# Attention times V in two groups of three head pairs per tile instead of three groups of two, with one eviction for each group

## The chip, the cores and the metric

The kernel runs on one core of a Trainium2 chip. The core has five engines that run at the same time, each through its own queue of instructions in order: TensorE (PE, matrix products; its weight loads are shown as PEld), VectorE (DVE), ScalarE (ACT), GpSimd (POOL) and SyncE (SP, which here only issues DMA transfers). Products land in PSUM, which has eight banks of 128 partitions by 512 fp32 columns; another engine has to copy ("evict") them to SBUF before the bank can be used again. The metric is the device time of one execution in microseconds (us); lower is better.

## What is computed

The reference is a chain of three stages over 4 batches, 12 heads, 448 positions and 64 elements per head:

```python
scores = scale * np.matmul(q, k.transpose(0, 1, 3, 2))
scores = np.einsum('bhij,hg->bgij', scores, w_pre)      # heads mixed
attn = softmax(scores)                                   # over j
attn = np.einsum('bhij,hg->bgij', attn, w_post)          # heads mixed again
x = np.matmul(attn, v)                                   # to 1792 tokens x 768
...                                                      # top-1 mixture of 8 experts, 768 -> 1024 -> 768
...                                                      # h = x @ w_in; (h - tanh(h)) @ w_out
```

The change lies in the last product of the attention, `attn @ v`.

## The kernel before

**Tiles and blocks.** Each batch is cut into four tiles of 120, 120, 120 and 88 query rows, so there are 16 tiles T = 0 to 15, all 12 heads together. A tile is cut into blocks of ten query rows times twelve heads, which fill 120 partitions: 12 blocks in a wide tile, 9 in a narrow one (T = 3, 7, 11, 15), 180 in all. Block s belongs to one step s of the loop over blocks.

**One step.** At step s the program issues, in this order: evictions that were left over from the last step (`flush`); P(s), the mixing of heads before the softmax, on TensorE; the maximum over each row on VectorE (L371); the scaled post-mixing matrix w of block s-1 (`emit_W`, L381 to L384, VectorE); at most one "fill" on TensorE (below); the exponential of block s on ScalarE (L374); on some steps a piece of the conversion of the last stage's weights (L115 to L117 on VectorE, L118 to L120 on POOL); T(s-2), the mixing after the softmax together with a transposition, on TensorE (L406), and its eviction on ScalarE (L411); then the other fills of the step. A step with no fill is called bare below.

**Fills.** The rest of the attention's TensorE work is put on given steps by hand: `emit_S2` (scores of two head pairs, for the tile after next), `tr_q` and `tr_k` (transpositions of q and k, split into two fp32r halves by ScalarE and VectorE), `emit_AV2` (attention times V) and `emit_X` (a product that lays a tile's result out as tokens and gives the router's logits). `at(pos, ...)` sets a fill on step int(pos); `at_e` takes the next step that no other fill of bank "e" has. P has two banks ("b"), T two ("c", which the router's small products also use), `emit_S2` takes four banks ("a" as two, "d", "e"), AV has the one bank "d", and tr_q, tr_k and X share the one bank "e". `run_fill` leaves the evictions of AV, tr_q, tr_k and X for later: those of "d" go to ScalarE just before T's eviction of the same step, or at the start of the next step if the fill stood behind T; those of "e" at the start of the next step.

**Attention times V.** For tile T and one pair of heads, eight fp32 products (four chunks of 112 positions, two heads, one in each half of the array's columns) write 128 partitions by 120 (88) columns of bank "d". A profile shows each fp32 product as two records. Two pairs make a group of 32 records with one eviction of 128x240 (128x176). With f the first block of tile T+1, the groups for pairs 0, 2 and 4 stand on steps f+3, f+7 and f+11 if tile T+1 has twelve blocks, on f+3, f+6 and f+9 if it has nine (`posAV`, LAG is 2). The last tile's AV comes after the loop, pair by pair, and is not touched by the change.

**What hangs on those places.** X of tile T goes on the first free steps from one and two steps behind the last group. For each batch (and for the last batch in two parts) the router's work `emit_R` follows X(T, 1) at fixed distances: part 0 (VectorE), then parts 1 and 2 (small products; positions in their queue on VectorE, up to L525), then parts 3 and 4 (small products; sums on VectorE). The store of a tile's tokens is issued on SP's queue behind X's eviction, among the relays L354 that bring scores from one layout to the other eight steps ahead.

**The last steps.** From step 173 on the first expert's weights are loaded, and on steps 175 to 178 they are split (`do1`): a cast on VectorE (L637) and a subtraction on POOL (L639). After the loop come the last X and AV products, the last router group, the experts and the two dense layers.

Of the kernel before, what the change touches and what calls it, by code (L numbers as in the profile page):

```python
# [30 lines left out]
def body(ctx: ExitStack, tc, q, k, v, w_pre, w_post, emb, tau, w1, w2, win, wout, out):  # L31
    nc = tc.nc
    pe, act, dve, pool, sp = nc.tensor, nc.scalar, nc.vector, nc.gpsimd, nc.sync
# [6 lines left out]
    NP = H // 2  # L40
# [13 lines left out]
    def ps(tag, nm):  # L54
        if len(PB) > 1:
            tag = {"a": "h", "b": "h"}.get(tag, "o")
        return psum[-1].tile([128, 512], F32, tag=tag, name=nm, bufs=PB[-1][tag])
# [67 lines left out]
    if True:  # L125
# [165 lines left out]
        def tr_q(T, hf, tag="e"):  # L291
            n = IT[T % 4][1]
            src = nat["q", T]
            pt = ps(tag, f"ptq{T}_{hf}")
            for p in range(3):
                pp = 3 * hf + p
                pe.transpose(pt[:, p * 120:p * 120 + n], src[:n, 2 * pp:2 * pp + 2, :].rearrange("p h d -> p (h d)"), ident[:n, :n])
            pv = pt[:, :360].rearrange("p (c i) -> p c i", c=3)[:, :, :n]
            hi = ap.tile([128, 3, 120], F32R, tag=f"qh{hf}", name=f"qh{T}_{hf}", bufs=1)
            lo = ap.tile([128, 3, 120], F32R, tag=f"ql{hf}", name=f"ql{T}_{hf}", bufs=1)  # L300
            qT[T, hf] = (hi, lo)

            def evac():
                act.copy(hi[:, :, :n], pv)
                return lambda: dve.tensor_sub(lo[:, :, :n], pv, hi[:, :, :n].bitcast(F32))
            return evac
# [56 lines left out]
        def emit_P(i):  # L363
            n = 12 * blocks[i][2]
            t = sr.pop(i)
            pt = ps("b", f"P{i}")
            pe.matmul(pt[:n, :S], wpre[:n, :n], t[:n, :], start=True, stop=True)  # L367

            flush2()
            mx = a2.tile([120, 4], F32, tag="mx", name=f"mx{i}", bufs=5)  # L370
            dve.tensor_reduce(mx[:n, 0:1], pt[:n, :S], op=ALU.max, axis=AX.X, negate=True)  # L371
            p = a2.tile([120, S], F32, tag="p", name=f"p{i}", bufs=LAG + 1)
            pj[i] = (p, mx)
            return lambda: act.activation(p[:n, :], pt[:n, :S], AF.Exp, bias=mx[:n, 0:1], scale=1.0, accum_out=mx[:n, 1:2])  # L374
# [3 lines left out]
        def emit_W(i):  # L378
            n = 12 * blocks[i][2]
            p, mx = pj[i]  # L380
            dve.tensor_scalar_add(mx[:n, 2:3], mx[:n, 1:2], 1e-9)  # L381
            dve.reciprocal(mx[:n, 3:4], mx[:n, 2:3])
            w = a2.tile([120, 120], F32, tag="w", name=f"w{i}", bufs=3)
            dve.tensor_scalar_mul(w[:n, :], wpost[:n, :], mx[:n, 3:4])  # L384
            wj[i] = w
# [4 lines left out]
        def emit_T(i):  # L390
            T, r, m = blocks[i]
            n = 12 * m
            b, it = divmod(T, 4)
            if r == 0:
                A[T] = aA.tile([CP, NJ, H, 120], F32, tag="A", name=f"A{T}", bufs=2)
            p, mx = pj.pop(i)
            w = wj.pop(i)
            wv = w.rearrange("p (g i) -> p g i", i=10)[:n, :, :m]
            pt = ps("c", f"T{i}")
            pv = pt[:CP, :NJ * n].rearrange("p (c g i) -> p c g i", c=NJ, i=m)  # L400
            tev[i] = (pt, pv, p, w, wv, n, m)
# [7 lines left out]
        def emit_TE(i):  # L409
            T, r, m = blocks[i]  # L410
            act.copy(A[T][:, :, :, 10 * r:10 * r + m], tev.pop(i)[1])  # L411
# [3 lines left out]
        def emit_AV(T, p, cpy=act.copy, m=1):  # L415
            b, it = divmod(T, 4)
            n = IT[it][1]
            if p == 0:
                xT[T] = cp.tile([128, KD, 120], F32, tag="xT", name=f"xT{T}", bufs=2)
            pt = ps("d", f"AV{T}_{p}")  # L420
            for x in range(m):
                for c in range(NJ):
                    for hh in range(2):
                        pe.matmul(pt[64 * hh:64 * hh + 64, x * 120:x * 120 + n], vt[b, p + x][:, hh, c, :],  # L424
                                  A[T][:, c, 2 * (p + x) + hh, :n], start=c == 0, stop=c == NJ - 1)
            return lambda: cpy(xT[T][:, p:p + m, :n], pt[:, :m * 120].rearrange("d (x i) -> d x i", x=m)[:, :, :n])
# [8 lines left out]
                e1()  # L435
            return evac

        def emit_AV2(T, p):
            return emit_AV(T, p, act.copy, 2)

        ssk = cp.tile([128, 4 * B], F32, name="ssk")
        lk = cp.tile([128, 4 * B, E], F32, name="lk")
# [171 lines left out]
    with mctx:  # L614
# [240 lines left out]
        def at(pos, fn, *a):  # L855
            side.setdefault(int(pos), []).append((fn, a))
# [3 lines left out]
        def at_e(pos, fn, *a):  # L860
            pos = int(pos)
            while pos in eused:
                pos += 1
            eused.add(pos)
            at(pos, fn, *a)
            return pos
# [5 lines left out]
        def posS2(T, p):  # L872
            return posS(T, p - p % 2 + 0.5)

        def posAV(T, p):
            f, nb = first[T + 1], ntile[T + 1]
            return f + LAG + 1 + p * nb / 6
# [17 lines left out]
        for b in range(1, B):  # L895
            for p in range(NP):
                e = posS2(4 * b - 1, p) + 1
# [3 lines left out]
            for b in range(B):  # L901
                at(posAV(4 * b - 1, p) + 2 if b else 1 + p, load_v, b, p)
        for T in range(4 * B - 1):
            for p in range(0, NP, 2):
                at(posAV(T, p), emit_AV2, T, p)
            e = posAV(T, NP - 2)
            if T == 4 * B - 2:
                continue
            at_e(e + 1, emit_X, T, 0)
            e = at_e(e + 2, emit_X, T, 1) - 2  # L910
            for gi, (_, t1) in enumerate(RG[:-1]):
                if t1 == T + 1:
                    for x, y in enumerate((0, 2, 2, 4, 4)):
                        at(e + 5 + y, emit_R, gi, x)
# [24 lines left out]
        def relay_to(i):  # L939
            while nxt[0] <= min(i, NBK - 1) and blocks[nxt[0]][0] in sdone:  # L940
                emit_relay(nxt[0])
                nxt[0] += 1
# [4 lines left out]
        def flush(tag=None):  # L947
            keep = []
            while late:
                x = late.pop(0)  # L950
                if tag in (None, x[0]):
                    y = x[1]()
                    if x[0] == "e" and callable(y):
                        late2.append((x[0], y))
                else:
                    keep.append(x)
            late.extend(keep)
            if tag:
                flush2(tag)
# [7 lines left out]
                    x[1]()  # L967

        def run_fill(fn, a):
            tag = "d" if fn is emit_AV2 else "e"  # L970
            if fn is emit_S2:
                flush("d")
                flush("e")
            elif fn is not emit_S:
                flush(tag)
            e = fn(*a)
            if fn in (emit_S, emit_S2):
                e()
                if a[1] + (fn is emit_S2) == NP - 1:
                    sdone.add(a[0])  # L980
            else:
                late.append((tag, e))
# [18 lines left out]
        prep_w()  # L1001
        relay_to(NSR - 1)
        at_e(4, tr_en)
        PEF = (tr_q, tr_k, emit_S, emit_S2, emit_AV2, emit_X, tr_en)
        for fn in [f() for f in (tr_q(1, 0, "e"), tr_q(1, 1, "d"))]:
            fn()
        for p in range(3):
# [5 lines left out]
        for s in range(NBK + LAG + 6):  # L1013
            todo = side.get(s, [])
            fill = [x for x in todo if x[0] in PEF]
            for fn, a in todo:
                if fn in (load_q, load_k, load_v, conv_load, zero_fill):
                    fn(*a)
            flush()
            relay_to(s + NSR - 1)  # L1020
            ex = emit_P(s) if s < NBK else lambda: None
            if 0 <= s - 1 < NBK:
                emit_W(s - 1)
            for fn, a in todo:
                if fn is emit_R and a[1] in (0, 1, 3):
                    fn(*a)
            i = s - LAG
            on = 0 <= i < NBK
            fill.sort(key=lambda x: x[0] not in (emit_S, emit_S2, emit_AV2))
            if fill and fill[0][0] in (emit_S, emit_S2, emit_AV2):  # L1030
                run_fill(*fill.pop(0))
            ex()
            for fn, a in todo:
                if fn is conv_do:
                    fn(*a)
            if on:
                emit_T(i)
                T_mm(i, 0, NJ)
                flush("d")
                emit_TE(i)  # L1040
            for x in fill:
                run_fill(*x)
            for fn, a in todo:
                if fn in (to_experts, do1) or fn is emit_R and a[1] in (2, 4):
                    fn(*a)
# [334 lines left out]
```

## Time and profile before

| | |
|---|---|
| median of 3 runs | 1373.29 us (1369.13 to 1375.64) |
| the profiled execution: its own time | 1376.32 us |
| the profiled execution: its span, first to last instruction | 1374.6 us |
| mean granted TensorE clock, as a share of full speed | 0.977 |
| TensorE busy over the span | 96% |
| VectorE, ScalarE, POOL busy | 74%, 54%, 37% |

The steps of the attention run from 24 us to about 518 us of the span. "Busy" of TensorE counts the time from a product's start to its modelled end; products overlap, so lengths of steps are best read from the starts of successive P products, not from busy times.

### The profile page before, as it was taken

Reading aid. Unit: us, or ns where it says so; the run is one execution under the profiler, and the core shown is the slowest. Engines: PE = TensorE matmul, PEld = TensorE weight load, DVE = VectorE, ACT = ScalarE, POOL = GpSimd, SP = SyncE. Lnnn points to the kernel's source line nnn. Section 1 sums busy time; section 2 is a strip of 40 time slices with the busy share of each in tenths; the row PEclk is TensorE's granted clock in tenths of the full one; section 3 lists DMA queues with packets and bytes.
Section 4 is the critical chain, followed back from the end, with each engine's and each line's share of the span. In section 5 each row is a group of like instructions: output and inputs, shape, how many; then the busy total and the mean of one; then the engine's idle time right before and its main releaser. Section 6 shows DMA issues by size and latency. Waiting matters only on the chain. (4 is left out here: it accounts for less than half of the span.)

```text
span 1374.6 us, 24956 instructions
## 1 busy us (share of the span) xinstructions
PE 1312.8 (96%) x9104; PEld 1146.0 (83%) x9104; DVE 1017.7 (74%) x2189; ACT 736.7 (54%) x1518; POOL 502.8 (37%) x495
## 2 busy tenths in 40 slices
PE   7999999999999987999999997899999989999998
PEld 5777776776777766999999996699998889999998
DVE  4776787678677773677776764688888788788886
ACT  5666666675666653545444453554444444544441
POOL 0233333333333323333332422544454334444432
PEclk9999999999999997999999999799999999999999
DMA  6886675667556564778877872421113133121102
GB/s 153 247 253 190 185 209 168 170 201 202 160 173 204 164 205 147 263 253 262 273 233 238 254 220 84 136 69 47 46 48 109 37 96 107 67 61 55 47 24 81
DMA packets 149412, 210.90 MB, mean 153 GB/s; under 512 B 54022, under 2 KB 109494, under 8 KB 149286
## 3 DMA queue, kind: packets, MB, share of 16 engines
q1 hardware_dynamic: 145104, 194.19, 46.4%
q0 software_dynamic: 2640, 12.19, 2.8%
q10 hardware_dynamic: 1542, 2.89, 0.7%
q8 instruction: 73, 1.20, 0.4%
q14 instruction: 53, 0.43, 0.1%
HBM read 135.70 MB, written 35.00 MB: 124 GB/s over the span
## 5 line engine op out<-in xcount | busy, mean ns | idle before, releaser
L406 PEld LDWEIGHTS T<-w,p 120*112 120x112 f32 (+1 forms) x1440 | 166.4, 177 | 66.8 <-issue 44.5
L120 POOL TENSOR_TENSOR cm<-cm,ct 128x256 f32<-128x256 f32 x96 | 70.1, 731 | 404.9 <-DVE ct L117 360.9
L406 PE MATMUL T<-w,p 120*112 120x120 f32 (+1 forms) x1440 | 185.6, 272 | 6.2 <-DVE w L384 3.0
L374 ACT ACTIVATE p<-P,mx 120x448 f32<-120x448 f32 x180 | 114.0, 633 | 119.8 <-DVE mx L381 106.3
L1220 POOL TENSOR_TENSOR gl<-th,gh 128x448 fp32r<-128x448 f32 x64 | 74.8, 1169 | 261.0 <-ACT gh L1219 192.6
L367 PE MATMUL P<-sr,wpre 120*120 120x448 f32 x360 | 166.2, 544 | 1.4 <-ACT p L374 1.4
L1271 PE MATMUL o<-woh,gh 128*128 128x384 f32 x448 | 152.5, 340 | 5.3 <-DVE acc L1277 5.3
L1240 ACT ACTIVATE u<-h 128x448 f32<-128x448 f32 x64 | 34.9, 546 | 222.9 <-PE h L1236 219.2
L1272 PE MATMUL o<-wol,gh 128*128 128x384 f32 x448 | 150.7, 336 | 0.0
L1273 PE MATMUL o<-woh,gl 128*128 128x384 f32 x448 | 150.7, 336 | 0.0
L371 DVE TENSOR_REDUCE mx<-P 120x1 f32<-120x448 f32 x180 | 111.4, 619 | 49.4 <-PE P L367 48.6
L1236 PE MATMUL h<-yh,wil 128*128 128x448 f32 x384 | 143.8, 374 | 3.3 <-POOL wil L1209 3.3
L1234 PE MATMUL h<-yh,wih 128*128 128x448 f32 x384 | 144.0, 375 | 1.1 <-ACT wih L1208 0.6
L1277 DVE TENSOR_TENSOR acc<-acc,o 128x384 f32<-128x384 f32 x196 | 106.9, 548 | 51.4 <-PE o L1273 51.4
L1235 PE MATMUL h<-yl,wih 128*128 128x448 f32 x384 | 143.9, 375 | 0.5 <-DVE yl L1183 0.5
L411 ACT COPY A<-T 112x480 f32<-112x480 f32 x180 | 101.5, 564 | 16.2 <-PE T L406 15.6
L686 PE MATMUL hi<-xhi,w1hi 128*128 128x256 f32 x384 | 108.8, 283 | 0.0
L687 PE MATMUL hi<-xli,w1hi 128*128 128x256 f32 x384 | 108.6, 283 | 0.0
L688 PE MATMUL hi<-xhi,w1li 128*128 128x256 f32 x384 | 108.4, 282 | 0.0
L424 PEld LDWEIGHTS AV<-A,v 112*64 112x64 f32 x1536 | 74.8, 138 | 23.9 <-issue 10.5
L669 PE MATMUL ypi<-w2hi,hhi 128*128 128x384 f32 x272 | 93.2, 343 | 0.1
L670 PE MATMUL ypi<-w2li,hhi 128*128 128x384 f32 x272 | 92.1, 338 | 0.6 <-DVE w2li L639 0.3
(223 smaller groups left out, 3279.9 us busy)
## 6 DMA issues: line engine op xcount, KB each, us to landing
sr<-ssb SPq DMA_DIRECT2D x176, 210.0 KB
r<-in_moe_w SPq DMA_DIRECT2D x72, 384.0 KB
r<-in_moe_w SPq DMA_DIRECT2D x52, 512.0 KB
craw<-in_moe_w_in SPq DMA_DIRECT2D x48, 256.0 KB
craw<-in_moe_w_out SPq DMA_DIRECT2D x48, 256.0 KB
raw<-wi_d SPq DMA_DIRECT2D x15, 768.0 KB
wor<-wo_d SPq DMA_DIRECT2D x15, 768.0 KB
wi_d<-cm SPq DMA_DIRECT2D x48, 128.0 KB
```

The lines of the kernel that those rows point to most:

```text
L367: pe.matmul(pt[:n, :S], wpre[:n, :n], t[:n, :], start=True, stop=True)
L371: dve.tensor_reduce(mx[:n, 0:1], pt[:n, :S], op=ALU.max, axis=AX.X, negate=True)
L374: return lambda: act.activation(p[:n, :], pt[:n, :S], AF.Exp, bias=mx[:n, 0:1], scale=1.0, accum_out=mx[:n, 1:2])
L406: pe.matmul(pt[:CP, c * n:(c + 1) * n] if m == 10 else pv[:, c], p[:n, c * CP:(c + 1) * CP], w[:n, :] if m == 10 else wv, start=True, stop ...
L686: pe.matmul(pt[:, :256], wh[:, sl], xh[:, c, :], start=c == 0, stop=False)
L687: pe.matmul(pt[:, :256], wh[:, sl], xl[:, c, :], start=False, stop=False)
L1234: pe.matmul(pt[:, :S], wi[0][:, c, sl], yh[:, c, :], start=c == 0, stop=False)
L1235: pe.matmul(pt[:, :S], wi[0][:, c, sl], yl[:, c, :], start=False, stop=False)
L1236: pe.matmul(pt[:, :S], wi[1][:, c, sl], yh[:, c, :], start=False, stop=c == KD - 1)
L1271: pe.matmul(pt[:, :384], gh[:, sl], wo[0][:, f, n0:n0 + 384], start=f == 0, stop=False)
L1272: pe.matmul(pt[:, :384], gh[:, sl], wo[1][:, f, n0:n0 + 384], start=False, stop=False)
L1273: pe.matmul(pt[:, :384], gl[:, sl], wo[0][:, f, n0:n0 + 384], start=False, stop=f == GF - 1)
```

## The change

The groups of attention times V take three pairs of heads each: 48 records into 360 of bank "d"'s 512 columns, and one eviction of 128x360 (128x264). A tile has two groups, for pairs 0 and 3, on steps f+3 and f+9 if tile T+1 has twelve blocks, on f+3 and f+7 if it has nine. The same products are issued in the same order. As the last group stands two steps earlier (at f+9 for f+11, or f+7 for f+9), X starts from two steps earlier too, and so does the router's work where X moved. The loads of v keep their steps.

```diff
-        def emit_AV2(T, p):
-            return emit_AV(T, p, act.copy, 2)
+        def emit_AV3(T, p):
+            return emit_AV(T, p, act.copy, 3)
...
         for T in range(4 * B - 1):
-            for p in range(0, NP, 2):
-                at(posAV(T, p), emit_AV2, T, p)
-            e = posAV(T, NP - 2)
+            for p in range(0, NP, 3):
+                at(posAV(T, p), emit_AV3, T, p)
+            e = posAV(T, NP - 3)
             if T == 4 * B - 2:
                 continue
             at_e(e + 1, emit_X, T, 0)
             e = at_e(e + 2, emit_X, T, 1) - 2
```

The other lines of the diff put the new name in the place of the old one where `run_fill` and the loop tell kinds of fills apart.

## Rows read from the trace of the kernel before

**Rows 1.** The page, busy us (share of the span) and instructions by engine

```profile
PE 1312.8 (96%) x9104; PEld 1146.0 (83%) x9104; DVE 1017.7 (74%) x2189; ACT 736.7 (54%) x1518; POOL 502.8 (37%) x495
```

**Rows 2.** Busy time by window: length, PE, PEld, DVE, ACT, POOL, clock, DMA, GB/s

```profile
24.00:480.00 456.00, 449.79 (x3855) 332.16 (x3856) 337.50 (x1049) 306.01 (x728) 155.31 (x216) 1.00 0.67 195
497.60:518.00 20.40, 15.77 (x141) 12.50 (x140) 16.41 (x42) 7.66 (x19) 9.40 (x4) 0.92 0.77 266
```

**Rows 3.** Groups by line and shape: xcount, busy us, mean ns, idle before

```profile
L426 ACT COPY xT<-AV 128x240 f32<-128x240 f32 x36 | 12.7, 353 | 11.2 <-PE AV L424 11.2
L462 ACT COPY raw<-X 120x384 f32<-120x384 f32 x24 | 11.6, 483 | 1.6 <-PE X L458 0.8
```

**Rows 4.** Timeline of PE, steps 174 (with AV) and 175 (bare): start, us

```profile
494.05 0.92 PE L367 MATMUL P<-sr,wpre 120*120 120x448 f32 x2
494.89 1.86 PE L424 MATMUL AV<-A,v 112*64 112x120 f32 x32
496.69 1.07 PE L406 MATMUL T<-w,p 120*112 120x120 f32 x8
497.60 0.92 PE L367 MATMUL P<-sr,wpre 120*120 120x448 f32 x2
...
499.17 0.92 PE L367 MATMUL P<-sr,wpre 120*120 120x448 f32 x2
```

**Rows 5.** Timeline of weight loads: step 53, bare, before T; step 68, before AV

```profile
163.40 0.79 PEld L406 LDWEIGHTS T<-w,p 120*112 120x112 f32 x7 [0.20 <-issue]
...
202.41 1.63 PEld L424 LDWEIGHTS AV<-A,v 112*64 112x64 f32 x32 [0.66 <-issue]
```

**Rows 6.** Timeline of PE, P of steps 54 (with S2) and 55

```profile
164.21 0.92 PE L367 MATMUL P<-sr,wpre 120*120 120x448 f32 x2
...
167.38 0.92 PE L367 MATMUL P<-sr,wpre 120*120 120x448 f32 x2
```

**Rows 7.** Timeline of DVE, steps 33 and 52: maximum, w, conversion, a slow w

```profile
106.55 0.62 DVE L371 TENSOR_REDUCE mx<-P 120x1 f32<-120x448 f32 x1 [0.94 <-PE P L367]
...
107.47 0.28 DVE L384 TENSOR_SCALAR w<-wpost,mx 120x120 f32<-120x120 f32 x1
...
108.44 0.42 DVE L117 SCALAR_TENSOR_TENSOR ct<-craw,ct 128x256 int32<-128x256 int32 x1
...
161.74 0.69 DVE L384 TENSOR_SCALAR w<-wpost,mx 120x120 f32<-120x120 f32 x1
```

**Rows 8.** Timeline of PE around bank "e", steps 24, 34 and 35

```profile
79.15 0.94 PE L367 MATMUL P<-sr,wpre 120*120 120x448 f32 x2
...
80.75 0.55 PE L281 MATMUL ptk<-ident,natk 112*128 112x112 f32 x4
...
107.47 0.92 PE L367 MATMUL P<-sr,wpre 120*120 120x448 f32 x2
...
109.42 0.60 PE L281 MATMUL ptk<-ident,natk 112*128 112x112 f32 x4 [0.21 <-DVE ql L305]
...
112.32 0.46 PE L324 MATMUL S<-kh,qh 64*120 64x448 f32 x1 [0.53 <-DVE kl L288]
```

**Rows 9.** Timeline around the second router group, P of steps 111 and 112

```profile
320.57 0.18 DVE L517 TENSOR_TENSOR pos<-R,carry 128x32 f32<-128x32 f32 x1
...
321.84 1.60 DVE L525 TENSOR_SCALAR p<-iota_s,posk 128x256 f16<-128x256 f32 x4
321.98 0.92 PE L367 MATMUL P<-sr,wpre 120*120 120x448 f32 x2
...
326.55 0.92 PE L367 MATMUL P<-sr,wpre 120*120 120x448 f32 x2
```

**Rows 10.** Timeline of the last steps, DVE and PE

```profile
502.51 1.74 DVE L384 TENSOR_SCALAR w<-wpost,mx 120x120 f32<-120x120 f32 x1
...
511.88 1.05 PE L406 MATMUL T<-w,p 120*112 120x120 f32 x8 [2.16 <-DVE w L384]
...
512.86 2.88 PE L424 MATMUL AV<-A,v 112*64 112x120 f32 x32
```

More of the change, by code (lines that the diff above doesn't have):

```diff
@@ L969, in run_fill @@
         def run_fill(fn, a):
-            tag = "d" if fn is emit_AV2 else "e"
+            tag = "d" if fn is emit_AV3 else "e"
             if fn is emit_S2:
@@ L1003, in body @@
         at_e(4, tr_en)
-        PEF = (tr_q, tr_k, emit_S, emit_S2, emit_AV2, emit_X, tr_en)
+        PEF = (tr_q, tr_k, emit_S, emit_S2, emit_AV3, emit_X, tr_en)
         for fn in [f() for f in (tr_q(1, 0, "e"), tr_q(1, 1, "d"))]:
@@ L1028, in body @@
             on = 0 <= i < NBK
-            fill.sort(key=lambda x: x[0] not in (emit_S, emit_S2, emit_AV2))
-            if fill and fill[0][0] in (emit_S, emit_S2, emit_AV2):
+            fill.sort(key=lambda x: x[0] not in (emit_S, emit_S2, emit_AV3))
+            if fill and fill[0][0] in (emit_S, emit_S2, emit_AV3):
                 run_fill(*fill.pop(0))
```

## The prediction

> **What bounds the kernel now.** I read the page first, for the engines' shares, then the busy times by window, then the timeline step by step. The page shows TensorE busy for 96% of the span and ScalarE, which does the evictions that the change merges, for 54% [rows 1]. The windows show that this holds in the attention itself: from 24 to 480 us TensorE is busy for 449.79 of 456.00 us, at a granted clock of 1.00 (2.4 GHz), ScalarE for 306 [rows 2]. So for most of the loop the length of a step is the TensorE work in it, and an eviction is worth something only where TensorE waits for it. The whole idle time of TensorE there is 6.2 us. The last steps are another stage: from 497.6 to 518 us TensorE idles 4.6 of 20.4 us and VectorE is the fullest engine [rows 2].
>
> The timeline gives a price list, since steps of one kind have almost one length. Between starts of successive P products a bare step takes 1.57 us, one with an AV group 3.55 [rows 4], one with S2 3.17 [rows 6].
>
> **The change part by part.**
>
> *Fewer group boundaries on TensorE.* A group of two pairs costs 3.55 - 1.57 = 1.98 us, of which 1.80 (496.69 - 494.89) are the stream of its 32 records and 0.18 the way into and out of it [rows 4]. The stream goes with the records, so three pairs cost 48/32 x 1.80 + 0.18 = 2.88. A wide tile now pays 2 x 2.88 = 5.76 for 3 x 1.98 = 5.94: 0.18 less. I take the same for the narrow ones. The fifteenth tile lies in the last steps, so 14 x 0.18 = -2.5 us. Bounds: nothing, if the boundary only turns up between other neighbours; and 14 x (0.66 - 0.20) = -6.4 if all that a group's first weight load waits beyond one in a bare step [rows 5] counts.
>
> *Evictions.* 45 copies of 240 or 176 columns become 30 of 360 or 264. The 240-column copy takes 0.353 us, a 384-column copy out of PSUM 0.483 [rows 3]; between them 360 columns come to 0.46. Three of the one against two of the other: 1.06 for 0.92 us a wide tile, 15 x 0.14 = 2 us of ScalarE. I cost it at nothing. What hides it is TensorE, the fuller engine. The longer copy stands ahead of T's eviction on ScalarE, 0.1 later; T has two banks and a step's time in hand, and a step with AV leaves ScalarE idle. Bank "d" is asked for again by the next S2 or AV at least a step later. Without that cover it would be at most 0.1 x 30 = 3 us, as a loss, and 2 us as a gain.
>
> *Steps that lose their AV.* This speaks against the change. Two groups of each tile's three leave their steps, 30 in all, and one new place is filled, at f+9, in seven tiles together with an S2. An AV group gave the other engines 2 us to catch up. Where the neighbours are bare or short, TensorE may now wait in two ways.
>
> (a) Bank "e". In step 24 tr_k starts 80.75 - 79.15 = 1.60 us after P, because the tr_q ahead of it stood in a step with AV; in step 34, behind a tr_q without AV, it starts after 109.42 - 107.47 = 1.95, having waited for VectorE's half of the split [rows 8]. With the modelled ends I price such a handover at 0.45. Going through the list of places, such pairs are new at steps 22 to 24, 30/31, 67 to 69, 75/76, 112 to 114 and 120/121, and go at 33/34, 78/79 and 123/124, which now have an AV in front. Three of the six have two handovers in a row, where the first delay gives the second its cover in part. I take 4.5 net, +2.0 us. Bounds: 0, and 6 x 0.78 = 4.7 by the worst case, an S2 that waits for VectorE just behind a tr_k (0.53 idle [rows 8], near 0.8 in the length of that step).
>
> (b) w. T of block s needs the w that VectorE makes behind the maximum of block s+1. VectorE's share of a step is the maximum, which starts about a us behind P, and w at once behind it: from 106.55 to 107.47 + 0.2 = 107.67, 1.1 us [rows 7]. As T(s) stands only behind P(s+2), two bare steps leave it some 0.2 us in hand by this count. A conversion takes it until 108.86, 1.2 more [rows 7], and pushes the next maximum back. With AV in the next step that cost nothing. Now a short or bare step stands between a conversion and the T at 18 to 20, 51 to 53, 96 to 98 and 165 to 167. By the queue T is 0.1 to 0.7 late, the more when POOL runs: w's scaling then takes 0.69 [rows 7] for 0.28. I take 4 x 0.3 = +1.2. Bounds 0 and 2.8.
>
> The Trainium skill has the reason for that row (SBUF — State Buffer, "Who interferes with whom"): a VectorE scaling in its two-port mode and a GpSimd instruction lock each other out for a whole instruction. The trace agrees in kind, 0.69 for 0.28 here and 1.74 in the last steps beside a POOL subtraction [rows 7, 10]. By the rule each of the four places could wait for a whole POOL instruction, at most the 1.74 - 0.28 = 1.46 of the last steps, and the sum would be up to 4 x (1.46 - 0.3) = 4.6 us higher.
>
> *The router's work, two steps earlier.* Parts 1 and 2 move from a step with AV to a step with S2 (62, 107, 152), followed by a bare step. Part 2 occupies VectorE from 320.57 to 323.44, 2.9 us [rows 9]; as POOL worked beside it there, I take 1.9 to 2.9, the lower end an estimate. From the start of the S2 step TensorE reaches the T that needs its w after 3.17 + 0.2 (part 1) + 1.57 + 0.85 + 0.3 (part 3) = 6.1. VectorE evicts S2 until 3.3, does part 2 until 5.2 to 6.2, then maximum and w until 6.4 to 7.4. T is 0.3 to 1.3 late, and 1.4 to 2.4 where a conversion lies between (107, 152): 0.7 + 1.9 + 1.9 = 4.5, and about 0.7 for a "c" bank that part 4 frees late. Today's three groups wait too: step 111 takes 4.57 [rows 9] against 3.17 for a step with S2 and 0.2 of products, 1.2 of wait, and all three about 3. Net +2.2. Bounds: -3 (today's waits go, none come) and +4.
>
> *The last steps.* Here POOL's subtraction holds w's scaling at 1.74 us and T waits up to 2.16 for w [rows 10]. Three router parts stand in steps 175, 177 and 179, the first with seven small VectorE operations of about 0.2 [rows 9]; two steps earlier those fall in front of the jam, -1.4. AV 14 ran at 174, 177 and 180, partly inside the waits; now it runs at 174 (+0.9, TensorE is full there) and 178 (inside a wait). The group at 180 ends at 512.86 + 2.88 = 515.7 [rows 10] and holds back the last two T's; by the pace of w there (0.62 + 1.74 + about 0.6, 3.0 from the last T at 511.88) they could start at 514.9: -0.8. Sum -1.3. Bounds: all 4.6 of idle [rows 2] and the 1.0 that AV lost to a lower clock (2.88 us for 1.86 [rows 4, 10]) back, less 0.9: -4.7; or AV3 at 178 wholly at 1.2 GHz, +2.7.
>
> *Queues.* X's token store moves with X on SP's queue, where the relays behind it run eight steps ahead; the loads of v find their buffers free no later than now. Both at nothing; a late relay would stop P, which shows nowhere in that stretch.
>
> Sum: -2.5 + 0 + 2.0 + 1.2 + 2.2 - 1.3 = +1.6. The profiled execution of 1376.32 us would become 1377.9, its span 1376.2. It lies 3.0 above the median of the three runs, 1373.29, so I predict 1374.9 us for the median.
>
> **Rivals.**
>
> *A: the savings come through, the waits don't (faster).* For it: the attention has only 6.2 us of idle now [rows 2], so queues seem loose. Place: the last steps. All of their bound, -4.7, with the boundaries at -2.5 and nothing lost elsewhere gives 1373.3 - 7.2 = 1366.1. It decides from -6.9 on. Against it: the lower bound of every other term is needed at once.
>
> *B: the stripped steps wait (slower).* VectorE, 337 us busy of 456 [rows 2], is late for bank "e" and w in all 30 steps without their AV. At the 0.45 of (a) this is 13.5, with the boundaries 1373.3 + 11.0 = 1384.3. It decides from (6.9 + 2.5)/30 = 0.31 us per stripped step on. For it: (a) and (b) are real waits. Against it: most stripped steps have an S2 or X beside them, whose T is covered.
>
> *C: the clock falls.* In the last steps, with TensorE idle by 23%, the granted clock is 0.92 [rows 2], so partly at 1.2 GHz. Two pockets of idle more in the loop that bring TensorE from 2.4 to 1.2 GHz would cost about what AV lost in step 180, 1.0 [rows 10], each for a step or two: 1376.9, still near. The Trainium skill warns of it (TensorE: Matmul & The Clock Gate, "A second HAM failure mode: psum-queue depth-cycling"): small idles between groups of products can bring the slow state back. The trace shows 1.00 from 24 to 480 us in spite of such idles.
>
> That the change does not do what it says I leave out: three times 120 columns fit the bank's 512.
>
> **How the numbers follow.** About 0.5%, 6.9 us, is what a measurement of this kernel can tell from no change. Chances: forecast, within 0.5%, 0.82, with C inside it; A 0.07; B 0.11. All lower bounds together make -14, all upper ones +14; neither is likely; one or two of them at a time, with the spread of a median of three runs (6.5 us between the runs of before), give 1367 to 1382.
>
> **What would show it.** L426 has 30 copies on ScalarE at about 0.46 us; steps with a wide AV alone take 4.45 us; TensorE's idle from 24 us to step 173 grows by some 3 us, under L288, L305 and L384 as releasers; the T's of steps 64, 109 and 154 wait for w; the last steps end 1 to 2 us earlier after P(175). Wrong would make it: waits of 0.3 us or more in most stripped steps, a P that waits for a relay, a clock below 1.00 in the loop, or AV3 groups that take clearly more or less than 1.5 times the stream of AV2.

## The result and the profile after

The changed kernel takes 1384.42 us (median of 6 runs, 1382.63 to 1388.42) against 1371.24 us of the kernel before, run beside it (6 runs, 1369.13 to 1375.64). The ratio is 1.0102, with a 95% interval of 1.0086 to 1.0118: about 13 us slower. The forecast was 1374.9 us with a range of 1367 to 1382: 1.6 us slower than the median then known (1373.29). So its sign was right and its size far too small. Rival B, the other one on the slower side, named 1384.3.

The engines do the same work as before [rows 1]. The page, busy time by engine:

```profile
PE 1314.3 (95%) x9104; PEld 1144.8 (83%) x9104; DVE 1018.6 (74%) x2189; ACT 736.6 (53%) x1503; POOL 503.2 (36%) x495
```

TensorE's busy time grew by 1.5 us, and ScalarE has 15 instructions fewer and no less busy time. So the time lies in gaps. The same stretch as in [rows 2], by window (length, PE, PEld, DVE, ACT, POOL, clock, DMA, GB/s):

```profile
24.00:480.00 456.00, 439.37 (x3715) 324.46 (x3716) 325.76 (x1014) 294.20 (x690) 150.09 (x209) 0.99 0.64 190
```

TensorE idles 16.6 us there instead of 6.2, and all the other engines got through less work. What it waited for between 24 and 480 us, from the view of waits (engine, line, releaser: us in total, times, longest):

```profile
PE S L324 <- DVE kl L288: 4.6, 9, 0.6
PE T L406 <- ACT A L411: 4.3, 4, 1.6
PE T L406 <- DVE w L384: 1.7, 3, 0.6
PE X L458 <- DVE ql L305: 1.5, 6, 0.3
...
PE ptk L281 <- DVE ql L305: 1.2, 4, 0.3
PE ptq L297 <- DVE kl L288: 0.9, 3, 0.3
PE M L533 <- DVE p L525: 0.8, 4, 0.2
```

No wait is long. There are many, and they stand behind four things: the second half of the split of k or q (kl, ql), T's eviction on ScalarE (A), the matrix w, and the router's one-hot rows (p).

**The account by steps.** Ends of products are modelled, so these idle times are too small. The whole loss is seen in the starts of successive P products. I give each step a price without waits, from steps that don't wait: 1.57 us bare; S2 adds 1.60, X 0.70, tr_q 0.31, tr_k 0.39, the router's small products of one step 0.10, a group of two pairs 1.98 (narrow tile 1.55), a group of three 2.80 (2.16). The wait of a step is its length less this price. From P(12) to P(174), which holds the AV of fourteen tiles, and from there to X(14,0):

| | length | prices | waits | behind tr_q, tr_k | for w | router | other | P(174) to X(14,0) |
|---|---|---|---|---|---|---|---|---|
| before | 445.5 | 434.5 | 10.9 | 6.6 | 0.2 | 3.2 | 0.9 | 23.9 |
| after | 463.4 | 429.8 | 33.7 | 17.9 | 3.4 | 11.3 | 1.1 | 22.4 |
| difference | +18.0 | -4.7 | +22.7 | +11.3 | +3.3 | +8.1 | +0.1 | -1.5 |

The sum is +16.5 us. P(12) started 2.3 us earlier in this execution (46.27 for 48.59; between 45.96 and 48.90 in the profiles of this study), so X(14,0) came 14.1 us later, which is near the 13.2 of the medians. Behind X(14,0), where the change touches nothing, the profiled execution after was 6.0 us shorter, so the two spans (1374.6 and 1382.7) differ by 8.1 only. The profiled execution of the kernel before lay 5.1 us above the median of its six runs (1376.32 for 1371.24); the part on why the prediction was wrong comes back to this.

**The group of three.** A step of a wide tile with nothing but the group, from the timeline of TensorE (start, length):

```profile
135.82 0.92 PE L367 MATMUL P<-sr,wpre 120*120 120x448 f32 x2
136.67 2.68 PE L424 MATMUL AV<-A,v 112*64 112x120 f32 x48
139.28 1.07 PE L406 MATMUL T<-w,p 120*112 120x120 f32 x8
140.19 0.92 PE L367 MATMUL P<-sr,wpre 96*96 96x448 f32 x2
```

The step takes 140.19 - 135.82 = 4.37 us, so a group costs 2.80, of which 139.28 - 136.67 = 2.61 are its stream. Two such groups are 0.34 us cheaper than three of two. The evictions are the 30 copies that were expected (groups by line and shape):

```profile
L426 ACT COPY xT<-AV 128x360 f32<-128x360 f32 x24 | 11.0, 460 | 24.6 <-PE AV L424 24.6
L426 ACT COPY xT<-AV 128x264 f32<-128x264 f32 x6 | 2.3, 379 | 4.4 <-PE AV L424 4.4
```

**Behind a tr_q.** In step 56 (P at 172.27) the kernel before had an AV group; now only tr_q stands there, and X in step 57 (P at 174.16). Timelines of TensorE, ScalarE and VectorE:

```profile
173.85 0.47 PE L297 MATMUL ptq<-ident,natq 120*128 120x120 f32 x3
174.16 0.92 PE L367 MATMUL P<-sr,wpre 120*120 120x448 f32 x2
...
176.22 0.93 PE L458 MATMUL X<-ien,xT 128*88 128x136 f32 x6 [0.29 <-DVE ql L305]
...
174.06 0.63 ACT L374 ACTIVATE p<-P,mx 120x448 f32<-120x448 f32 x1 [0.84 <-DVE mx L381]
...
174.68 0.56 ACT L411 COPY A<-T 112x480 f32<-112x480 f32 x1
175.13 0.47 ACT L304 CAST qh<-ptq 128x360 fp32r<-128x360 f32 x1
...
175.63 0.53 DVE L305 TENSOR_TENSOR ql<-ptq,qh 128x360 fp32r<-128x360 f32 x1 [0.83 <-ACT qh L304]
```

Read it as one chain. ScalarE's queue is in order: exponential of step 56 (which waits for the maximum), T's eviction, and only then the first half of the split (qh); VectorE's half (ql) waits for that, X for ql. tr_q ends at 174.32, but qh starts at 175.13. The kernel before, with the AV group of a narrow tile in the step (1.55 us longer; P(57) at 172.39):

```profile
171.29 0.64 ACT L374 ACTIVATE p<-P,mx 120x448 f32<-120x448 f32 x1 [1.04 <-DVE mx L381]
...
172.08 0.47 PE L297 MATMUL ptq<-ident,natq 120*128 120x120 f32 x3
...
172.74 0.46 ACT L304 CAST qh<-ptq 128x360 fp32r<-128x360 f32 x1
...
173.96 0.86 PE L458 MATMUL X<-ien,xT 128*88 128x136 f32 x6
```

There the exponential is done before tr_q runs, qh starts 0.19 us behind the end of tr_q instead of 0.81, and X starts 1.57 us after P(57) instead of 2.06. The same happens to S2 behind a tr_k, where it costs a whole 1.0 us of step 32.

**For w.** Step 53 (P at 162.31), VectorE and TensorE:

```profile
161.67 0.42 DVE L117 SCALAR_TENSOR_TENSOR ct<-craw,ct 128x256 int32<-128x256 int32 x1
...
162.01 0.62 DVE L371 TENSOR_REDUCE mx<-P 120x1 f32<-120x448 f32 x1
...
162.92 0.69 DVE L384 TENSOR_SCALAR w<-wpost,mx 120x120 f32<-120x120 f32 x1
...
163.76 1.05 PE L406 MATMUL T<-w,p 120*112 120x120 f32 x8 [0.54 <-DVE w L384]
```

A conversion holds the maximum of step 52 until 162.01; w with 0.69 us follows, and T comes 0.76 us late by the price list. Step 167 (P at 493.55) waits 0.66, with a w of 0.28 us, but the maximum in front starts only with P and not 0.30 us before it (VectorE):

```profile
493.56 0.62 DVE L371 TENSOR_REDUCE mx<-P 120x1 f32<-120x448 f32 x1
...
494.47 0.28 DVE L384 TENSOR_SCALAR w<-wpost,mx 120x120 f32<-120x120 f32 x1
```

**The router.** Its second group, VectorE's part 2 in step 107 and what follows (VectorE, ScalarE, TensorE):

```profile
321.77 0.18 DVE L517 TENSOR_TENSOR pos<-R,carry 128x32 f32<-128x32 f32 x1
...
323.03 1.60 DVE L525 TENSOR_SCALAR p<-iota_s,posk 128x256 f16<-128x256 f32 x4
324.56 0.61 DVE L371 TENSOR_REDUCE mx<-P 120x1 f32<-120x448 f32 x1
...
325.26 0.64 ACT L374 ACTIVATE p<-P,mx 120x448 f32<-120x448 f32 x1 [3.37 <-DVE mx L381]
...
325.46 0.28 DVE L384 TENSOR_SCALAR w<-wpost,mx 120x120 f32<-120x120 f32 x1
...
325.89 0.56 ACT L411 COPY A<-T 112x480 f32<-112x480 f32 x1
...
326.50 1.07 PE L406 MATMUL T<-w,p 120*112 120x120 f32 x8 [1.60 <-ACT A L411]
...
327.81 1.75 PE L367 MATMUL P<-sr,wpre 120*120 120x448 f32 x2
329.35 1.72 PE L406 MATMUL T<-w,p 120*112 120x120 f32 x8
330.91 0.92 PE L367 MATMUL P<-sr,wpre 120*120 120x448 f32 x2
```

P(108) was there from 320.88 on, but its maximum starts at 324.56, behind part 2. The exponential waits 3.37 us for it, and T(106)'s eviction stands behind that exponential on ScalarE though its data had been ready; so the bank that T(107) needs comes free 1.6 us late (the router's products M stand between the two T's and took the other one of the two banks "c"). T(107)'s w was there at 325.46 + 0.28 = 325.74, 0.76 us before T(107) starts. As T starts 0.15 us behind its w in step 53, some 0.6 us of this wait are the bank's alone; the rest is part 2, which holds up both. P(109) starts at 322.86 and P(110) at 327.81: 4.95 us for a step priced at 1.98. Then P and T take almost twice their time. By window:

```profile
324.00:326.00 2.00, 0.60 (x6) 0.32 (x6) 1.93 (x7) 0.74 (x3) 0.23 (x1) 1.00 0.67 241
326.00:328.00 2.00, 1.50 (x12) 1.50 (x13) 1.86 (x8) 1.49 (x4) 0.00 (x0) 0.86 0.78 253
328.00:330.00 2.00, 2.00 (x7) 1.14 (x6) 1.59 (x4) 0.45 (x2) 1.79 (x3) 0.50 0.32 107
...
458.00:460.00 2.00, 0.79 (x7) 0.79 (x8) 1.78 (x8) 1.82 (x5) 0.00 (x0) 1.00 0.67 254
460.00:462.00 2.00, 2.00 (x10) 1.18 (x9) 0.49 (x2) 0.84 (x2) 0.00 (x0) 0.64 0.83 252
```

After TensorE was busy for only 0.60 of 2 us, the granted clock falls to 0.50, which is 1.2 GHz, and step 110, bare, takes 3.10 instead of 1.57. The third group shows the same (0.79 of 2 us busy, then a clock of 0.64; step 155, from 460.36 on, takes 1.4 us too long). In no other stretch of 8 us between 24 and 480 us is the clock below 1.00, and in the kernel before in none.

### The profile page after: what moved, and what is told of

The parts are those of the page before. It is cut to its first block, busy times and chain, and to the rows that moved or that the text cites. A ratio compares the mean times of both kernels' runs of the same rounds, so it can differ in the third digit from the quotient of the medians.

```text
span 1382.7 us, 24937 instructions
## 1 busy us (share of the span) xinstructions
PE 1314.3 (95%) x9104; PEld 1144.8 (83%) x9104; DVE 1018.6 (74%) x2189; ACT 736.6 (53%) x1503; POOL 503.2 (36%) x495
## 5 line engine op out<-in xcount | busy, mean ns | idle before, releaser
L119 POOL TENSOR_SCALAR cm<-cm 128x256 f32<-128x256 f32 x96 | 88.4, 921 | 8.4
```

## The experiments

Two theories stood at first. V: the steps that lost their AV group uncover waits in the queues of VectorE and ScalarE, each at its own place, and the loss is their sum. M: it is the move of X and of the router two steps earlier that costs, not the groups. Each kernel ran beside the kernel before; ratios are to that. Where an expectation gives a sum of waits, it counts the steps up to P(179), by which the change has 37.9 us and the kernel before 13.7; the results below count to P(174), as in the table above.

**X and the router at their old places.**

```diff
-            e = posAV(T, NP - 3)
+            e = posAV(T, NP - 2)
```

> The changed kernel (1384.4 us) with one thing undone: X, and the router's work behind it, stand again where they stood before the change; the AV groups of three pairs stay. Theory V (VectorE's work of transpositions, w's and router meets steps too short to hide it, since the AV that covered them has gone): the seven X's that now wait 0.45 to 0.55 us for bank "e" lose that, -3.5; the router's part 2 comes back to a step that no longer has an AV, so it still waits some 2 us a group, together about -3. In all -6 us, 1376 to 1380 us. Rival G (the larger group itself costs, through its one bank or its longer eviction, wherever its neighbours stand): nothing changes, 1383 to 1386 us. Rival M (the move of X and of the router is the whole loss): back to the kernel before less the saved boundaries, 1367 to 1372 us.

Measured: 1387.46 us, ratio 1.0123 [1.0095, 1.0151]: no better than the change, a miss. The router's waits fell from 11.3 to 8.3 us, but the waits behind tr_q and tr_k stayed (18.2 for 17.9): X left steps 45, 90 and 135 and now waits 1.0 us in steps 57, 102 and 159. From P(174) to X(14,0) it takes 24.7 us, so the 1.5 us of the last steps are gone too and 0.8 more are lost. M alone is out: at the old places the loss is as large.

**The router's VectorE part under the longest step.** Parts 1 and 2 go to steps 66, 111 and 156, which hold S2 and a group of three.

```diff
-                    for x, y in enumerate((0, 2, 2, 4, 4)):
+                    for x, y in enumerate((0, 6, 6, 8, 8) if gi < 3 else (0, 2, 2, 4, 4)):
```

> The changed kernel with the router's parts 1 and 2 of the first three groups moved from the S2 step in front of a bare step to the step with S2 and AV3 (66, 111, 156), parts 3 and 4 two steps behind that; all else as changed. Theory V: the steps 64, 108 to 110 and 153 to 155, which now hold 10.7 us of wait, fall to about their price list, and about 1.5 us of wait is left: 1374 to 1377 us. Rival G: the router has nothing to do with it, 1383 to 1386 us. If the router waits for something other than cover (its bank "c", say), the wait moves along with it: 1382 to 1386 us.

Measured: 1377.90 us, ratio 1.0059 [1.0038, 1.0079], 6.5 us faster than the change, 0.9 above the time expected. The router's waits went from 11.3 to 1.0 us, with 0.9 back at each of steps 69 and 114. Nothing else was touched, so these waits are shown to come from the router's place.

**Another bank for tr_q.** In bank "d", where no AV stands any more, instead of "e".

```diff
-            at_e(posS2(T, 0) - 2, tr_q, T, 0)
-            at_e(posS2(T, 2) - 2, tr_q, T, 1)
+            at_e(posS2(T, 0) - 2, tr_q, T, 0, "d")
+            at_e(posS2(T, 2) - 2, tr_q, T, 1, "e" if T in (4, 8, 12) else "d")
...
```

> The changed kernel with the transpositions of q in bank "d" instead of "e", but for the three that share a step with an AV group. So tr_q, tr_k and X no longer hand one bank on to each other in neighbouring steps. If the one bank is what turns VectorE's lateness into a wait of TensorE, the waits at steps 23, 24, 31, 45, 57, 68, 69, 76, 90, 102, 113, 114, 121, 135, 147, 159 (8.4 us together) go: 1375 to 1378 us; those of S2 behind tr_k (25, 32, 70, 77, 115, 122) and of the router stay. If VectorE is late in any case, TensorE waits for w or for the next S2 instead, and less than 2 us is gained: 1382 to 1386 us. Rival G: nothing changes or the busier bank "d" costs more.

Measured: 1386.50 us, ratio 1.0103 [1.0073, 1.0132]: nothing gained. The waits left X and tr_k (step 45: 0.46 to 0.00; 57: 0.55 to 0.11) and came back at the next S2 (step 46: 0.09 to 0.56; 58: 0.15 to 0.60). Behind tr_q and tr_k they sum to 18.0 as before. Step 58 shows why (ScalarE and TensorE):

```profile
177.93 0.48 ACT L462 COPY raw<-X 88x384 f32<-88x384 f32 x1
...
178.67 0.46 PE L324 MATMUL S<-kh,qh 64*120 64x448 f32 x1 [0.15 <-DVE lg L463]
```

S2 takes bank "e" too, which X of step 57 now holds, and X's eviction stands in the same late queue: X ends at 176.76, its copy starts at 177.93, and lg, the part of the eviction on VectorE, releases S2. So a second bank for tr_q alone moves the wait to the next fill. That the banks have no part in it is not shown, since S2 needs both "d" and "e".

**Conversions on long steps.** Each piece of the weights' conversion goes to a step with S2 or AV, instead of an even spread.

```diff
+        LONG = []
+        for s_ in range(12, 170):
+            fns = [x[0] for x in side.get(s_, [])]
+            LONG += [s_] * (fns.count(emit_S2) + fns.count(emit_AV3) + (emit_AV3 in fns and emit_X in fns))
...
-            st = 12 + (NBK - 24) * j // CA
+            st = LONG[j]
```

> The changed kernel with the 72 conversions of the attention stage moved onto the steps with an S2 or an AV group (two on a step that has both, or an AV group and an X), so that none stands on a bare or short step. Theory V: VectorE's 1.2 us per conversion is then covered; the waits for w (20, 53, 98, 167: 3.0 us) go, the handovers of bank "e" that follow a conversion shrink by half (-4 us), the router keeps or gains a little: 1375 to 1379 us. Rival, the bank alone: only the waits for w go, 1380 to 1383 us. Rival G: 1383 to 1386 us.

Measured: 1383.81 us, ratio 1.0083 [1.0053, 1.0113]. The waits for w fell from 3.4 to 0.4 us, so they are shown to come from the conversions in front. Step 53 in the timeline of TensorE now is a bare 162.40 - 160.82 = 1.58 us:

```profile
160.82 0.92 PE L367 MATMUL P<-sr,wpre 120*120 120x448 f32 x2
...
162.40 0.92 PE L367 MATMUL P<-sr,wpre 120*120 120x448 f32 x2
```

The waits behind tr_q and tr_k didn't move (17.8), which was a miss, and the router's rose to 14.0, as a conversion and the router's part now met in step 62. That rise ate the gain.

**The split ahead of T's eviction.** The reading of steps 56 and 57 above gave theory O: it is ScalarE's order that makes the split late.

```diff
                 flush("d")
+                if fill and fill[0][0] in (tr_q, tr_k):
+                    run_fill(*fill.pop(0))
+                    flush("e")
                 emit_TE(i)
```

> Theory O: the waits behind tr_q and tr_k (X, tr_k or S2 waiting for VectorE's half of the split) come from the order of ScalarE's queue: exponential of the step, T's eviction of 0.45 us, and only then the first half of the split, so that the whole chain up to bank e being free is served 0.45 us late. With the first half ahead of T's eviction each of the 18 waits of three batches at steps 23 to 35 and their like, and the seven in front of X, should fall by up to 0.45: 8 to 11 us off the step lengths, 1374 to 1377 us. Rival: VectorE is what is late (its maximum and w stand ahead of its half): the waits stay, and the time is 1383 to 1386.

Measured: 1380.16 us, ratio 1.0063 [1.0039, 1.0086]. The waits behind tr_q and tr_k fell from 17.9 to 9.4 us. Steps 56 and 57 again (P at 170.12 and 172.00):

```profile
171.90 0.63 ACT L374 ACTIVATE p<-P,mx 120x448 f32<-120x448 f32 x1 [0.84 <-DVE mx L381]
...
172.52 0.45 ACT L304 CAST qh<-ptq 128x360 fp32r<-128x360 f32 x1
172.86 0.58 ACT L411 COPY A<-T 112x480 f32<-112x480 f32 x1
...
173.00 0.53 DVE L305 TENSOR_TENSOR ql<-ptq,qh 128x360 fp32r<-128x360 f32 x1 [0.36 <-ACT qh L304]
...
173.61 0.91 PE L458 MATMUL X<-ien,xT 128*88 128x136 f32 x6
```

X starts 1.61 us after P(57) instead of 2.06, without a wait. O holds: 8.5 of the 17.9 us came from T's eviction standing in front of the split; of the other 9.4 no run tells the cause one by one. Expected were 8 to 11 us in all and 4.3 came, because the router's waits rose from 11.3 to 15.2. The wait itself is the same, 1.60 us of T for the eviction A in step 109 (in step 64 it rose from 0.98 to 1.59), but the clock now fell in all three groups, and sooner: 0.50 from 324 to 326 us and also from 194 to 196, where the first group stands and the change had 1.00.

**Two evictions for each group**, of two pairs and one.

```diff
...
+            def evac():
+                for x, m in ((0, 2), (2, 1)):
+                    act.copy(xT[T][:, p + x:p + x + m, :n], pt[:, x * 120:(x + m) * 120].rearrange("d (x i) -> d x i", x=m)[:, :, :n])
+            return evac
```

> The three pairs of a group are evicted by two copies, of two pairs and one, and all else is as in the changed kernel. Theory V (the loss lies in the steps that lost their AV group, not in the evictions): no change, 1383 to 1386, and the step lengths the same within 0.1 us. Rival: the merged eviction is part of the story (a longer copy is late for T's eviction or for bank d): a change of 2 us or more in either direction.

Measured: 1387.20 us, ratio 1.0119 [1.0093, 1.0144]; its interval overlaps that of the change, though the median lies 1.2 us above the band expected of no change. The steps from P(12) to P(174) take 464.0 us for 463.4, with the same waits but for the router's (11.9 for 11.3). Merging the evictions is worth no more than can be measured here.

**The kernel before with its router two steps earlier.** Groups of two pairs as they were.

```diff
-                        at(e + 5 + y, emit_R, gi, x)
+                        at(e + 3 + y, emit_R, gi, x)
```

> The kernel before with its groups of two pairs, and the router's five parts two steps earlier, as they stand after the change. Theory V: the router costs so much in the changed kernel because the step behind its VectorE part has also lost its AV group; with a group of two still in steps 64, 109 and 154 only the small products M wait, and the time is 1371 to 1375. Rival: the earlier place is enough by itself: the 7.8 us of router waits come back, 1377 to 1380.

Measured: 1368.79 us, ratio 0.9987 [0.9969, 1.0006], better than the 1371 to 1375 expected. The exponential behind part 2 waits its 3.37 us for the maximum here too, but an AV group runs meanwhile. The router's waits are 3.0 us (3.2 before), and from P(174) to X(14,0) it takes 21.6 us instead of 23.9. So the same move that cost 8 us in the changed kernel costs nothing with an AV group of two in steps 64, 109 and 154, and the gain of the last steps belongs to the router's move alone; the group of three takes 0.8 of it back.

**Three repairs together**: the router under the longest steps, the conversions on long steps (one, not two, on two of the router's three), the split ahead of T's eviction. The diffs are those above, but for the list of long steps, which starts at step 6.

> The changed kernel with three repairs: the router's parts 1 and 2 under the step with S2 and AV (as in the run with the router covered), the conversions on steps with S2 or AV, and the split of tr_q and tr_k ahead of T's eviction. If waits add up by their places (37.9 - 9.0 - 3.0 - 8 to 11 = 15 to 18, against 13.7 in the kernel before, with 3.0 less of product time): 1369 to 1374, level with the kernel before. Rival: a wait taken away turns up one step later, as with the second bank for tr_q: 1375 to 1380.

Measured: 1366.39 us, ratio 0.9968 [0.9952, 0.9985], 18 us faster than the change and better than the 1369 to 1374 expected. Waits 11.5 us, those for w 0.4, the router's 0.5. Of the 9.8 behind tr_q and tr_k, 3.4 stand in step 68, behind the one router step that has two conversions.

**One conversion there as well**, and the third moved to step 12.

> The three repairs as before, but with one conversion instead of two on the first of the three steps that also carry the router's VectorE part; the third conversion goes to step 12. In the run with two, step 68 waited 3.4 us, where its two sisters with one conversion waited 0.6. Theory V, waits by place: 2.9 us less than that run's 1366.4, so 1362 to 1365, and 0.993 to 0.996 of the kernel before. Rival: within 1 us of that run, 1365.5 to 1367.5, because the wait turns up in another place.

Measured: 1364.71 us, ratio 0.9957 [0.9944, 0.9971]. Step 68 waits 0.5 instead of 3.4. The median fell by 1.7 us for the 2.9 expected; it lies in the expected band. What TensorE still waits for between 24 and 480 us, and the window:

```profile
PE P L367 <- ACT p L374: 1.4, 1, 1.4
PE T L406 <- ACT A L411: 1.2, 5, 0.3
PE T L406 <- DVE w L384: 0.9, 3, 0.5
```

```profile
24.00:480.00 456.00, 452.30 (x3921) 338.25 (x3921) 347.09 (x1061) 309.01 (x722) 157.93 (x216) 1.00 0.66 197
```

**Groups of two with the split ahead of T's eviction**, and the router two steps earlier.

> The kernel before with its groups of two pairs, the router two steps earlier, and the split of tr_q and tr_k ahead of T's eviction: what the repairs give to groups of two. Its waits behind tr_q and tr_k are 6.6 us in all, and some 3 of them should go: 1364 to 1368. If groups of three are worth their shorter products (4.7 us of step lengths in fourteen tiles) once their waits are mended, this stays 1 to 4 us above the repaired groups of three. Rival: the repairs are the whole gain, and groups of two come out level with groups of three or below, 1361 to 1364.

Measured: 1363.66 us, ratio 0.9955 [0.9942, 0.9968]: the rival's time. Its waits behind tr_q and tr_k fell from 6.6 to 2.5. Both repaired kernels beat the two kernels of this study, and by these intervals they are level with each other.

| us | length P(12) to P(174) | prices | waits | P(174) to X(14,0) | median |
|---|---|---|---|---|---|
| groups of three, three repairs, one conversion each | 438.6 | 429.8 | 8.8 | 22.4 | 1364.7 |
| groups of two, order and router | 441.9 | 434.5 | 7.3 | 21.6 | 1363.7 |

## Why the prediction was wrong

*What bounds the kernel.* Right for the kernel before: TensorE's work sets the steps. But "an eviction is worth something only where TensorE waits for it" was taken to mean that little slack is needed where there is little waiting now. The 6.2 us of idle [rows 2] were small because each tile had three groups of 2 us in which the other queues caught up; they didn't say how late the queues would be without them.

*Boundaries: -2.5, measured -4.7.* The way into and out of a group is 0.19 us (2.80 - 2.61), as read. The stream of three is 2.61 and not 1.5 times 1.80, which saves another 0.09 a group. So a tile saves 0.34 and not 0.18, fourteen times.

*Evictions: 0.* Right in effect, by the run with two copies, and the copy took the 0.46 us that was estimated.

*(a) Bank "e": +2.0, measured +11.3.* The failed step. The price of one handover, 0.45, is what steps 23, 31 and 76 show (0.43 to 0.44). Its cause and the list of places were wrong. I listed pairs of tr_q and tr_k. Missing were the seven X behind a tr_q (steps 45, 57, 90, 102, 135, 147 and 159, about 0.5 each) and the three S2 behind a tr_k (32, 77 and 122, 1.0 each), 6 to 7 us together; the latter price stood in [rows 8] and I had it only as a worst case. Two handovers in a row didn't cover each other: 0.44 in step 23 and 0.74 in step 24. And the reason given, VectorE's half, is only the end of a chain that runs over ScalarE, as the run with the split ahead of T's eviction shows.

*(b) w: +1.2, measured +3.3, 3.0 of it at the four places.* The mechanism and the four places were right (20, 53, 98, 167), and a conversion in front is shown as the cause. The price of 0.3 was the middle of the queue's 0.1 to 0.7; 0.66 to 0.84 came, its upper end, in all four. The slow scaling has its part in it: in steps 20, 53 and 98 w took 0.69 us for 0.28, which put 0.41 more in front of T, beside a POOL product of the same conversion (L118, 162.93 to 163.54 in step 53). In step 167 w took 0.28 and T was hardly less late, since the maximum had started 0.3 later against P. The Trainium skill's rule that a VectorE scaling in its two-port mode and a GpSimd instruction lock each other out for a whole instruction (SBUF — State Buffer, "Who interferes with whom") agrees with the trace in kind, 0.69 for 0.28 beside that product of 0.61 us. The 1.46 us a place that the prediction took from the last steps as the most it could cost did not come.

*The router: +2.2, measured +8.1.* The other failed step, outside its bounds of -3 to +4. I followed VectorE to w and asked when T gets its w. What T(107) waited for was its bank: T(106)'s eviction stands on ScalarE behind an exponential that waits for a maximum, and that maximum stands behind part 2. I costed only the bank that part 4 frees, at 0.7 in all, and never wrote down ScalarE's order. The bank adds some 0.6 us in step 109, where 2.97 came for the 1.4 to 2.4 of the forecast, and steps 108 and 153 wait another 0.4 each. Some 2.9 of the 8.1 are the two bare steps behind it (110 and 155), slowed by the clock.

*The last steps: -1.3, measured -1.5.* Right, the wide group's cost of 0.8 included.

*The rivals.* A is out, as the time went the other way. B was right in kind: nearly all new waits stand in a stripped step or the one behind it, and 22.7 us over the 28 stripped steps of fourteen tiles are 0.8 each, far beyond its deciding point of 0.31. Its sum was not: 13.5 us of waits were too few, and its time fits by luck: the products saved more than it counted, the last steps gained, and its base of 1373.3 lay 2 us above the later median. Nor was it VectorE alone, but ScalarE's order as well. "Against it: most stripped steps have an S2 or X beside them, whose T is covered" was the wrong test: X and S2 are themselves what waits. C was real inside B, two pockets at 1.5 and 1.4 us, each near the 1.0 that it had priced. The Trainium skill's warning of small idles between groups of products (TensorE: Matmul & The Clock Gate, "A second HAM failure mode: psum-queue depth-cycling") agrees with the trace only in part: the clock fell to 0.50 behind the 1.60 us wait from 324.9 to 326.5 us, while the many small waits elsewhere, which are nearer to what it describes, left it at 1.00.

*What stays open.* With repairs, groups of three are 3.3 us shorter from P(12) to P(174) and 2.5 to X(14,0) than groups of two, but not in the median (1364.7 for 1363.7). In the two profiles P(12) starts 2.0 us later with groups of three (48.90 for 46.86), and the stage behind the attention takes longer: 832 us from the first expert product to the end, 829 with groups of two. In the kernel before it takes 836. This seems to go with the execution and not with the kernel: in the three profiled executions that lay 3 us or more above their kernel's median (before, router early, conversions on long steps) it takes 834 to 836 us, in the other nine 829 to 832. What makes it longer no run here tells, and whether groups of three are worth anything once repaired stays open.

## What to carry to other kernels

Before long fills are merged in a loop of many in-order engines, write down for each step that loses one what the other engines still have queued, engine by engine, with the instruction that each of them waits for; a wait is then at the consumer behind it, and giving one consumer another buffer only moved it here. A low idle time of the busiest engine says that the cover is enough as it stands, not that there is cover to spare. Here the same products in larger groups cost 13 us, and one changed order on ScalarE's queue, with the router moved, was worth 7 us without any larger group.

## What was not expected of the hardware

The stream of 48 records ran in 2.61 us, where 32 take 1.80, so a group's cost is not quite proportional to its records. And two stretches with TensorE busy for 0.60 and 0.79 of 2 us, in an attention that otherwise runs at 1.00, were followed by a lower granted clock (0.86 and 0.50, and 0.64), while waits of 0.3 to 1.0 us, spread over some thirty steps, never moved it.
